# One arena on chip for the loads of a fused attention, soft-MoE and MLP kernel

## The chip, the cores and the metric

One core of a Trainium2 chip runs the whole kernel. The metric is the device time in microseconds (us), median of the runs. All inputs and outputs are float32 in device memory.

## The reference

The inputs q, k, v have 8 batches, 8 heads, 576 positions, 64 features; p has 32 rows a head. Three stages follow each other:

```
# stage 1, attention through 32 packed rows (per batch and head)
pp  = softmax(scale * p @ k.T) @ v
x   = softmax(scale * q @ pp.T) @ pp        # x becomes [4608, 512]
# stage 2, soft mixture of 8 experts with 4 slots each
L   = x @ phi                               # [4608, 32]
si  = softmax(L, over the 4608 rows).T @ x  # [32, 512]
so  = for each expert e:  relu(si[e] @ w1[e]) @ w2[e]   # w1 512x1024, w2 1024x512
y   = softmax(L, over the 32 slots) @ so    # [4608, 512]
# stage 3, MLP with mish
out = mish(y @ w_in) @ w_out                # w_in 512x2048, w_out 2048x512
```

## The kernel before, in words

**Stage 1** goes batch by batch. The half batches of k and q arrive as tiles of 128 x 1152 floats (4608 B a partition), are transposed by VectorE (`tr_kq`, L329 and L335) and freed; v is read by `pv`. The remainder of v, `vr` (L131), has two buffers of its own. The logits go into the tile LT, [128, 8, 192]. At the end of the stage the slot inputs stand in SIT (L949).

**Stage 2** runs the experts in order. `ex_h(e)` multiplies SIT with the four tiles of w1[e] (L981, 16 matmul records) and ScalarE copies the result (h, L988). `ex_x(e)` transposes it by TensorE (L996) and VectorE (h1T, L1000, relu L1001). `ex_o(e)` multiplies with the four tiles of w2[e] (L1008, 16 records). Between the experts stand the softmax over the slots (`combine`, VectorE, ScalarE and GpSimd, L1031 to L1049), its transposes into CS (`combine_t`, L1060 and L1065), a few idle matmuls `warm` (L975), and the conversion of w_in (`conv`, `convs`: ScalarE L274, VectorE L280 and L283). w_in and w_out are loaded as pairs of 32-bit words and turned into float32 on the chip, into `win[0..7]`. Eight tiles of w_in are loaded ahead of the experts (EARLY) and converted at the end of stage 1 (`bg`); four more are dealt out in the queue after w2 of expert 2, two after w1 of expert 3, two after w2 of expert 3; the sixteen tiles of w_out come last.

**Stage 3** first folds the expert outputs into the first MLP matrix (SOT, `emit_mp` L1149, `emit_mr` L1157, result MS). Then it takes blocks of 256 rows and quarters of the hidden width: `emit_h` (L1201) gives hidden values, ScalarE applies mish into tile `s` (L1206), the value is split into a high and a low part (`emit_c`, L1225 to L1236), and `emit_o` (L1316) multiplies with the split w_out (`whi`, `wlo`). Steps from the third block on use a Strassen-like form with sums S (L1217) and precomputed T tiles (`build_t`), and `emit_store` collects the result in `osb` (L1357, L1363). In the first six steps the last tiles of w_out are converted and split beside it (`cl`, `cu`, `cz`: L1186, L1187, L276).

**The order of the loads.** All loads are issued by SyncE's queue in the order of the list `jobs`: k, v, q and p, 8 early tiles of w_in, then the weights. `plan()` fixes for each job which ring it goes to, and `pump()` emits the next load as soon as the former owner of its buffer has been freed in the program text, so a load that waits holds up all behind it. Before the change there are five kinds of slots, all of 4608 B: ring_a (7), ring_b (20), ring_p (3, only in stage 1), and four slots of ring_x which belong to the transposed k and q until the last batch is done. A weight tile fills 4096 B of such a slot. The first weights take a7, b15, x4, b5, in this order, which is 31; the next one needs a tile that expert 0 has read. Ten of ring_b are used a second time; then ring_b and LT are given up (after `ex_o(4)`), and CS, MS, whi and wlo take their place. Each pool says whether a new tile waits for whole pools or for the tiles that it lies over (`reuse_waits="tile"`). The order of the instructions on each engine is the order of the program text (`manual_schedule`).

Of the kernel before, what the change touches and what calls it, by code (L numbers as in the profile page):

```python
# [9 lines left out]
F32 = mybir.dt.float32  # L10
F32R = mybir.dt.float32r
# [8 lines left out]
def kernel(  # L20
# [25 lines left out]
    FT = FF // 128  # L46
    TB = 4 * B
    RA, RB, RX, RP = 7, 20, 4, 3
    NE, NB2 = 8, 10
    NL = 16  # L50

    const = ctx.enter_context(tc.tile_pool(name="const", bufs=1))
    ring_a = ctx.enter_context(tc.tile_pool(name="ring_a", bufs=RA))
    wg = ctx.enter_context(tc.tile_pool(name="wg", bufs=4, reuse_waits="tile"))
    b_ctx, p1 = ExitStack(), ExitStack()
    ring_x = ctx.enter_context(tc.tile_pool(name="ring_x", bufs=RX // 2, reuse_waits="tile"))
    ring_b = b_ctx.enter_context(tc.tile_pool(name="ring_b", bufs=RB, side="right"))
    lt_p = b_ctx.enter_context(tc.tile_pool(name="lt_p", bufs=1, side="right"))
    ctx.enter_context(tc.manual_schedule())


    jobs = []
    CV = [("wi", i) for i in range(16)] + [("wo", i) for i in range(16)]
    N_CV = {(2, 1): 4, (3, 0): 2, (3, 1): 2}
# [6 lines left out]
    slots = {0: [ring_a, RA, []], 1: [ring_b, RB, []], 2: [None, RX // 2, []], 3: [None, RX // 2, []], 4: [None, RP, []]}  # L71
    got = {}
    freed = set()
    N_QKV = 3 * HQ * B + 1 + NE
    order = []

    def plan():

        n = RA + RB - NE + RP
        order.extend(0 if (i - N_QKV + RP) % (RA + RB) < RA else 1 for i in range(N_QKV))  # L80
        order[N_QKV - RP:N_QKV] = [4] * RP
        cycle = [2, 3] * (RX // 2) + [0] * RA
        rest = [0] * RA + [1] * (n - RA) + cycle[0:RX] + [1] * (NE - RP) + [0] * RA + [1] * NB2 + 9 * cycle
        late = len(AFTER[E - 1, 1])
        order.extend(rest[0:len(jobs) - late - N_QKV] + [0] * RA + [2, 3] * (RX // 2) + [0] * (late - RA - RX))

    nxt = [0]

    def pump():
        while nxt[0] < len(jobs):  # L90
            name, emit = jobs[nxt[0]]
            pool, n, held = slots[order[nxt[0]]]
            if pool is None or len(held) >= n and held[-n] not in freed:
                return
            t = pool.tile([128, 18 * D], F32, tag=("ring0", "ring1", "kT", "qT", "ring4")[order[nxt[0]]], name="r_" + "_".join(map(str, name)))
            held.append(name)
            got[name] = t
            emit(t)
            nxt[0] += 1
# [111 lines left out]
    slots[4][0] = p1.enter_context(tc.tile_pool(name="ring_p", bufs=RP))  # L211
# [45 lines left out]
    LT = lt_p.tile([128, B, 192], F32, name="LT")  # L257
# [602 lines left out]
    slots[2][0] = slots[3][0] = ring_x  # L860
# [98 lines left out]
    wg2 = wp.enter_context(tc.tile_pool(name="wg2", bufs=4, reuse_waits="tile"))  # L959
    t2 = wp.enter_context(tc.tile_pool(name="t2", bufs=2, reuse_waits="tile"))  # L960
    two = ep.enter_context(tc.tile_pool(name="two", bufs=2, reuse_waits="tile"))
    win += [wg2.tile([128, 1024], F32, name=f"win{i}", tag="wg") for i in range(4, 8)]
# [129 lines left out]
    convs((3, 1), 0, 2)  # L1092
# [43 lines left out]
    blk = {}  # L1136
# [54 lines left out]
    def emit_h(n, c, z):  # L1191

        if not z:
            blk["m", n, c] = tp.tile([128, 4, 256], F32, name="s", tag="s"), None
        if "Z" in R:
            hp = ps_b.tile([128, 512], F32, name="h3", tag="h3", bufs=2)
        else:
            hp = ps_h.tile([128, 2, 512], F32, name="h3", tag="hp")[:, 0]
        for f in range(2):
            ft = 4 * c + 2 * z + f  # L1200
            nc.tensor.matmul(  # L1201
                hp[:, 256 * f:256 * f + 256], lhsT=MS[:, 128 * ft:128 * ft + 128], rhs=CS[:, 256 * n:256 * n + 256],
                start=True, stop=True,
            )
        s = blk["m", n, c][0][:, 2 * z:2 * z + 2]
        nc.scalar.activation(out=s, in_=hp.rearrange("p (f n) -> p f n", f=2), func=AF.Mish)  # L1206
# [39 lines left out]
    def build_t(c, ws=None):  # L1246
# [21 lines left out]
        if ws is None:  # L1268
            wa, wb = (g2.tile([128, 1024], F32, name=x, tag=x, bufs=2).rearrange("p (f n) -> p f n", f=2) for x in tags)
# [15 lines left out]
        else:  # L1285
            T4 = tp.tile([128, 2, 256], F32, name="T4", bufs=1)
# [128 lines left out]
    tp = ctx.enter_context(tc.tile_pool(name="tp", bufs=2, side="right", reuse_waits="tile"))  # L1415
# [111 lines left out]
```

## Time and profile before

| | us |
|---|---|
| median of 3 runs | 657.84 |
| the 3 runs | 655.38, 659.72, 657.84 |
| span of the profiled execution, first to last instruction | 652.8 |
| median less that span | 5.04 |

| engine | busy in the span, us |
|---|---|
| TensorE matmul (PE) | 613.1 |
| TensorE weight load (PEld) | 529.8 |
| VectorE (DVE) | 503.1 |
| ScalarE (ACT) | 339.2 |
| GpSimd (POOL) | 57.4 |

The profile gives no device time of the profiled execution apart from its span, so what lies around the span is known only as the difference of the second table line. Times below are us from the start of the span. SP is SyncE, whose queue issues the loads. Stage 1 ends at about 162 us, the experts at about 222, and the long second MLP product begins at about 241.

### The profile page before, as it was taken

Reading aid. Unit: us, or ns where it says so; the run is one execution under the profiler, and the core shown is the slowest. Engines: PE = TensorE matmul, PEld = TensorE weight load, DVE = VectorE, ACT = ScalarE, POOL = GpSimd, SP = SyncE. Lnnn points to the kernel's source line nnn. Section 1 sums busy time; section 2 is a strip of 40 time slices with the busy share of each in tenths; the row PEclk is TensorE's granted clock in tenths of the full one; section 3 lists DMA queues with packets and bytes.
Section 4 is the critical chain, followed back from the end, with each engine's and each line's share of the span. In section 5 each row is a group of like instructions: output and inputs, shape, how many; then the busy total and the mean of one; then the engine's idle time right before and its main releaser. Section 6 shows DMA issues by size and latency. Waiting matters only on the chain.

```text
span 652.8 us, 14427 instructions
## 1 busy us (share of the span) xinstructions
PE 613.1 (94%) x5878; PEld 529.8 (81%) x5878; DVE 503.1 (77%) x997; ACT 339.2 (52%) x681; POOL 57.4 (9%) x78
## 2 busy tenths in 40 slices
PE   7799999998879969999999999999999999999996
PEld 5577777676225538888899999999999999999996
DVE  5998888787561298988779987788778877887883
ACT  3345545645522376655456555555555555555551
POOL 5122222121040040000000000000000000000000
PEclk9999999999979989999999999999999999999999
DMA  8998956998899980011100110111011101110111
GB/s 287 316 306 300 330 162 228 403 398 312 308 400 400 396 321 16 1 33 32 33 18 17 34 33 2 33 35 33 2 33 33 33 2 33 33 33 2 33 34 33
DMA packets 42354, 89.61 MB, mean 137 GB/s; under 512 B 10928, under 2 KB 19248, under 8 KB 42288
## 3 DMA queue, kind: packets, MB, share of 16 engines
q1 hardware_dynamic: 41840, 88.36, 38.9%
q8 instruction: 46, 0.75, 0.5%
q10 hardware_dynamic: 192, 0.26, 0.2%
q14 instruction: 20, 0.16, 0.1%
q0 software_dynamic: 256, 0.07, 0.0%
HBM read 79.23 MB, written 9.44 MB: 136 GB/s over the span
## 4 chain that ended last, share of the span: by engine, by line
PE 69%; DVE 18%; ACT 5%; DMA 5%; issue 2%; SPq 0%; POOL 0%; DVEq 0%; ACTq 0%; POOLq 0%
PE o L1316 39%; PE so L1316 13%; PE h L1201 5%; DVE kT L329 5%; DMA r_w<-in_moe_w_dram 3%; DVE A L501 1%; PE so L1008 1%; PE s L367 1%; DVE mx L500 1%; PE cp L1060 1%; PE s L481 1%; DVE osb L1357 1%; PE hp L981 1%; DVE nmx L377 1%; DVE S L1217 1%
## 5 line engine op out<-in xcount | busy, mean ns | idle before, releaser
L1316 PE MATMUL o<-whi,gh 128*128 128x256 f32 (+1 forms) x444 | 117.5, 309 | 0.5 <-DVE osb L1357 0.5
L1316 PE MATMUL o<-wlo,gh 128*128 128x256 f32 (+1 forms) x444 | 116.6, 307 | 0.0
L1232 ACT CAST gh<-s 128x512 fp32r<-128x512 f32 x116 | 53.8, 512 | 110.1 <-PE o L1316 110.1
L1206 ACT ACTIVATE s<-h 128x512 f32<-128x512 f32 x144 | 83.7, 595 | 45.3 <-PE h L1201 44.9
L1316 PE MATMUL o<-whi,gl 128*128 128x256 f32 (+1 forms) x444 | 95.6, 305 | 0.0
L1316 PEld LDWEIGHTS o<-wlo,gh 128*128 128x128 f32 x444 | 84.3, 190 | 4.7
L1316 PEld LDWEIGHTS o<-whi,gh 128*128 128x128 f32 x444 | 83.4, 190 | 5.3 <-issue 1.8
L1235 DVE TENSOR_TENSOR gl<-s,gh 128x512 fp32r<-128x512 f32 x116 | 59.5, 554 | 35.3 <-ACT gh L1232 35.3
L1236 DVE TENSOR_TENSOR Sl<-S,Sh 128x1024 fp32r<-128x1024 f32 x58 | 71.0, 1224 | 10.6 <-ACT Sh L1233 9.1
L1316 PEld LDWEIGHTS o<-whi,gl 128*128 128x128 f32 x444 | 71.6, 189 | 4.6
L1316 PE MATMUL o<-T,Sh 128*128 128x256 f32 x464 | 73.9, 281 | 0.4 <-DVE osb L1357 0.4
L1233 ACT CAST Sh<-S 128x1024 fp32r<-128x1024 f32 x58 | 61.0, 1052 | 5.4 <-DVE S L1217 4.1
L1316 PEld LDWEIGHTS o<-T,Sh 128*128 128x128 f32 x464 | 63.1, 188 | 0.6 <-DVE osb L1357 0.6
L1217 DVE TENSOR_TENSOR S<-s 128x256 f32<-128x256 f32 x116 | 48.8, 421 | 10.5 <-ACT s L1206 10.5
L1201 PE MATMUL h<-CS,MS 128*128 128x256 f32 x288 | 55.8, 284 | 0.0
L1316 PE MATMUL o<-T,Sl 128*128 128x256 f32 x232 | 46.9, 284 | 0.0
L1201 PEld LDWEIGHTS h<-CS,MS 128*128 128x128 f32 x288 | 44.1, 188 | 2.2 <-issue 1.0
L1357 DVE TENSOR_TENSOR osb<-osb,o 128x256 f32<-128x256 f32 x86 | 33.1, 418 | 9.6 <-PE o L1316 6.6
L1316 PE MATMUL so<-T,Sh 128*128 128x256 f32 (+1 forms) x232 | 38.6, 289 | 0.3 <-DVE osb L1357 0.3
L367 PE MATMUL s<-kT,win 128*128 128x288 f32 x128 | 34.7, 414 | 4.5 <-ACT win L379 4.0
L1316 PEld LDWEIGHTS o<-T,Sl 128*128 128x128 f32 x232 | 35.9, 190 | 0.0
L329 DVE STREAM_TRANSPOSE kT<-r_k 128x512 f32<-128x512 f32 x32 | 32.5, 1092 | 2.2 <-DMA r_k<-in_k_dram 2.2
(254 smaller groups left out, 1122.8 us busy)
## 6 DMA issues: line engine op xcount, KB each, us to landing
r_w<-in_moe_w_dram SPq DMA_DIRECT2D x63, 512.0 KB, 10.4
r_k<-in_k_dram SPq DMA_DIRECT2D x16, 576.0 KB, 7.3
r_q<-in_q_dram SPq DMA_DIRECT2D x16, 576.0 KB, 4.8
r_v<-in_v_dram SPq DMA_DIRECT2D x64, 128.0 KB, 5.7
r_wi<-in_moe_w_in_dram SPq DMA_DIRECT2D x16, 512.0 KB, 9.4
r_wo<-in_moe_w_out_dram SPq DMA_DIRECT2D x16, 512.0 KB, 8.5
out_dram<-osb SPq DMA_DIRECT2D x64, 128.0 KB, 2.2
vr<-in_v_dram SPq DMA_DIRECT2D x16, 64.0 KB, 2.7
```

Source lines behind the costliest of these rows:

```text
L329: nc.vector.transpose(out=T[:, dh, main].rearrange("p (i r a) -> p a i r" if nm == "k" else "p (i a r) -> p a i r", i=4, a=4,), in_=x[:, 0 ...
L367: nc.tensor.matmul(ps[:, n, 0:288], lhsT=pBD[b % 2][:, hq, dh], rhs=kT[:, dh, 288 * n:288 * n + 288], start=(dh == 0), stop=(dh == 1),)
L377: nc.vector.tensor_reduce(out=nmx, in_=ps[:, :, 0:288], axis=AX.XY, op=ALU.max, negate=True)
L1201: nc.tensor.matmul(hp[:, 256 * f:256 * f + 256], lhsT=MS[:, 128 * ft:128 * ft + 128], rhs=CS[:, 256 * n:256 * n + 256], start=True, stop=True,
L1206: nc.scalar.activation(out=s, in_=hp.rearrange("p (f n) -> p f n", f=2), func=AF.Mish)
L1217: nc.vector.tensor_tensor(out=S[:, k], in0=x, in1=y, op=op)
L1232: nc.scalar.copy(out=gh[:, f, t], in_=s[:, f, t])
L1233: nc.scalar.copy(out=Sh, in_=S)
L1235: nc.vector.tensor_tensor(out=gl[:, f, t], in0=s[:, f, t], in1=gh[:, f, t].bitcast(F32), op=ALU.subtract)
L1236: nc.vector.tensor_tensor(out=Sl, in0=S, in1=Sh.bitcast(F32), op=ALU.subtract)
L1316: nc.tensor.matmul(o, lhsT=lhsT, rhs=rhs, start=first, stop=stop)
L1357: add = lambda o, x, y: nc.vector.tensor_tensor(out=o, in0=x, in1=y, op=ALU.add)
```

## The change

q, k, v tiles, the weights and several buffers of the MLP are cut out of one pool `arena` with three tiles: AW (18 weight tiles, 72 KB a partition), AC (5) and AY (4856 floats, its tail holds LT). Tiles of q, k, v lie in it at a pitch of 4608 B, weights at a pitch of 4096 B; a load now waits until every earlier owner whose range it overlaps has been freed. ring_b, ring_p, lt_p, wg2 and p3 are gone; ring_a (7) and ring_x (4) stay. In stage 1 there are 29 slots (y2, c4, w16, a7). The first weights take y3, c5, w18, x4, a7: 37; the next ones c5 and then AW again. CS takes the place of AC; MS, whi and wlo that of AW (W3), after the experts. `win[4..7]`, the later `s` and `osb` tiles and T4 lie in AY. Since `win[4]` lies on the first weight tile, `ex_h(0)` now stands ahead of the first two conversions. All four tiles of w_in after expert 3's w1 follow at once, rather than two there and two after its w2. The tile pool `tp` serves only the first six steps of the MLP.

```diff
-    RA, RB, RX, RP = 7, 20, 4, 3
-    NE, NB2 = 8, 10
-    NL = 16
+    RA, RX, RW, RC, RY = 7, 4, 18, 5, 3
+    NE, NL = 8, 16
...
+    arena = ctx.enter_context(tc.tile_pool(name="arena", bufs=1, side="right", reuse_waits="tile"))
+    AW, AC, AY = (arena.tile([128, n], F32, name=x, tag=x) for x, n in (("AW", 1024 * RW), ("AC", 1024 * RC), ("AY", 4856)))
+    LT = AY[:, 4856 - 192 * B:4856].rearrange("p (b c) -> p b c", b=B)
-    N_CV = {(2, 1): 4, (3, 0): 2, (3, 1): 2}
+    N_CV = {(2, 1): 4, (3, 0): 4}
...
+        a, x = [("a", i) for i in range(RA)], [("x", i) for i in range(RX)]
+        first = [(z, 18 * D * i) for z, n in (("y", 2), ("c", 4), ("w", 16)) for i in range(n)] + a
+        order.extend(first[(i - N_QKV) % len(first)] for i in range(N_QKV))
+        y, c, w = ([(z, 1024 * i) for i in range(n)] for z, n in (("y", RY), ("c", RC), ("w", RW)))
+        order.extend((y + c + w + x + a + c + 2 * w)[0:len(jobs) - late - N_QKV] + (a + x + a)[0:late])
...
+            if any(k == kind and lo < at + n and at < hi and who not in freed for k, lo, hi, who in used):
+                return
...
-    win += [wg2.tile([128, 1024], F32, name=f"win{i}", tag="wg") for i in range(4, 8)]
+    win += [AY[:, 1024 * i:1024 * i + 1024] for i in range(4)]
...
+    ex_h(0)
     convs((2, 1), 0, 2)
-    ex_h(0)
...
-    convs((3, 1), 0, 2)
+    convs((3, 0), 2, 4)
...
-    b_ctx.close()
-    p3 = ctx.enter_context(tc.tile_pool(name="p3", bufs=1, side="right", reuse_waits="tile"))
-    CS = p3.tile([128, NT], F32R, name="CS")
-    MS = p3.tile([128, FF], F32R, name="MS")
-    whi = p3.tile([128, FT, DM], F32R, name="whi")
-    wlo = p3.tile([128, FT, DM], F32R, name="wlo")
+    CS = arena.tile([128, NT], F32R, name="CS", tag="AC")
...
+            s = tp.tile([128, 1024], F32, name="s", tag="s") if steps.index((n, c)) < 6 else two_of("s")
...
-            T4 = tp.tile([128, 2, 256], F32, name="T4", bufs=1)
+            T4 = AY[:, 4096:4608].rearrange("p (f n) -> p f n", f=2)
...
-            osb = g2.tile([128, 2, 512], F32, name="osb", tag="osb", bufs=2)
+            osb = two_of("osb").rearrange("p (z n) -> p z n", z=2)
...
-    tp = ctx.enter_context(tc.tile_pool(name="tp", bufs=2, side="right", reuse_waits="tile"))
+    W3 = arena.tile([128, 1024 * RW], F32R, name="W3", tag="AW")
+    whi, wlo = (W3[:, FT * DM * i:FT * DM * (i + 1)].rearrange("p (f n) -> p f n", f=FT) for i in range(2))
+    MS = W3[:, 2 * FT * DM:]
+    tp = wp.enter_context(tc.tile_pool(name="tp", bufs=2, reuse_waits="tile"))
+    turn = {"s": 0, "osb": 0}
+    def two_of(x):
+        turn[x] ^= 1
+        i = (0 if x == "osb" else 2048) + 1024 * turn[x]
+        return AY[:, i:i + 1024]
```

## Rows read from the trace of the kernel before

**Rows 1.** Stretches: length, busy us of each engine (instructions), granted clock, DMA share, GB/s.
```profile
162.00:222.00 60.00, 50.89 (x662) 21.68 (x664) 25.34 (x59) 19.27 (x32) 8.03 (x9) 0.94 0.97 365
242.00:652.80 410.80, 404.25 (x3052) 386.98 (x3050) 329.44 (x630) 225.40 (x386) 0.00 (x0) 0.99 0.10 25
```

**Rows 2.** Waits of the queues: engine, line, waited for: total us, times, longest; after 242 us.
```profile
PE o L1316 <- DVE osb L1357: 0.9, 3, 0.4
```

**Rows 3.** Stretch around the end of stage 1, columns as in rows 1.
```profile
156.00:172.00 16.00, 13.86 (x163) 6.58 (x167) 9.79 (x26) 6.56 (x15) 0.00 (x0) 1.00 0.65 224
```

**Rows 4.** Timeline of SyncE's queue, 150 to 190 us: start, us, what.
```profile
151.10 13.31 SPq L138 DMA_DIRECT2D r_w<-in_moe_w_dram  x4
165.73 5.77 SPq L148 DMA_DIRECT2D r_w<-in_moe_w_dram  x4
```

**Rows 5.** Waits of TensorE, 160 to 224 us, columns as in rows 2.
```profile
PE so L1008 <- DVE h1T L1001: 6.7, 2, 5.5
...
PE xp L996 <- ACT h L988: 0.8, 1, 0.8
...
PE hp L981 <- DMA r_w<-in_moe_w_dram: 0.2, 1, 0.2
```

**Rows 6.** Timeline of TensorE, 160 to 224.5 us; in brackets idle before and its end.
```profile
169.00 1.92 PE L1008 MATMUL so<-r_w,h1T 128*32 128x512 f32 x16
...
182.81 3.64 PE L1008 MATMUL so<-r_w,h1T 128*32 128x512 f32 x16 [5.47 <-DVE h1T L1001]
...
194.86 1.34 PE L981 MATMUL hp<-r_w,SIT 128*32 128x512 f32 x6
196.44 1.48 PE L981 MATMUL hp<-r_w,SIT 128*32 128x512 f32 x9 [0.24 <-DMA r_w<-in_moe_w_dram]
...
197.75 0.59 PE L981 MATMUL hp<-r_w,SIT 128*32 128x512 f32 x1
...
219.30 3.34 PE L1008 MATMUL so<-r_w,h1T 128*32 128x512 f32 x20
```

**Rows 7.** The chain that ended last, in order of time: start, us, what.
```profile
186.90 9.50 DMA r_w<-in_moe_w_dram
...
211.83 9.72 DMA r_w<-in_moe_w_dram
```

**Rows 8.** Timeline of ScalarE, 159 to 178 us.
```profile
160.09 1.24 ACT L274 ACTIVATE win<-r_wi 128x512 f32<-128x512 f32 x2
164.26 1.01 ACT L988 COPY h<-hp 128x1024 f32<-128x1024 f32 x1 [2.93 <-PE hp L981]
165.91 1.01 ACT L988 COPY h<-hp 128x1024 f32<-128x1024 f32 x1 [0.64 <-PE hp L981]
...
173.75 3.02 ACT L274 ACTIVATE win<-r_wi 128x512 f32<-128x512 f32 x4
```

**Rows 9.** Timeline of VectorE, 160 to 183 us.
```profile
162.00 0.76 DVE L280 TENSOR_SCALAR r_wi<-r_wi 128x512 int32<-128x512 int32 x2
162.67 1.29 DVE L283 SCALAR_TENSOR_TENSOR win<-win,r_wi 128x512 int32<-128x512 int32 x2
...
174.47 1.77 DVE L283 SCALAR_TENSOR_TENSOR win<-win,r_wi 128x512 int32<-128x512 int32 x2 [2.88 <-ACT win L274]
...
181.04 0.43 DVE L1000 STREAM_TRANSPOSE h1T<-xp 128x256 f32<-128x256 f32 x1
```

**Rows 10.** Waits of SyncE's queue, 80 to 105 us, columns as in rows 2.
```profile
SPq L131 <- PE pv L419: 12.4, 2, 9.6
```

**Rows 11.** Waits of TensorE, 222 to 242 us, columns as in rows 2.
```profile
PE mp L1157 <- DVE msb L1152: 5.2, 1, 5.2
```

**Rows 12.** Timelines of ScalarE and TensorE, 246 to 253 us.
```profile
247.53 1.14 ACT L1186 CAST whi<-w 128x512 fp32r<-128x512 f32 x2
...
248.47 1.10 PE L1316 MATMUL o<-whi,gl 128*128 128x512 f32 x4
```

**Rows 13.** Stretch of the first MLP steps, columns as in rows 1.
```profile
262.00:282.00 20.00, 20.00 (x93) 16.33 (x93) 19.25 (x32) 12.10 (x21) 0.00 (x0) 1.00 0.00 1
```

More of the change, by code (lines that the diff above doesn't have):

```diff
@@ L54 @@
     wg = ctx.enter_context(tc.tile_pool(name="wg", bufs=4, reuse_waits="tile"))
-    b_ctx, p1 = ExitStack(), ExitStack()
+    p1 = ExitStack()
     ring_x = ctx.enter_context(tc.tile_pool(name="ring_x", bufs=RX // 2, reuse_waits="tile"))
-    ring_b = b_ctx.enter_context(tc.tile_pool(name="ring_b", bufs=RB, side="right"))
-    lt_p = b_ctx.enter_context(tc.tile_pool(name="lt_p", bufs=1, side="right"))
+    arena = ctx.enter_context(tc.tile_pool(name="arena", bufs=1, side="right", reuse_waits="tile"))
     ctx.enter_context(tc.manual_schedule())
+    AW, AC, AY = (arena.tile([128, n], F32, name=x, tag=x) for x, n in (("AW", 1024 * RW), ("AC", 1024 * RC), ("AY", 4856)))
+    LT = AY[:, 4856 - 192 * B:4856].rearrange("p (b c) -> p b c", b=B)
     jobs = []
     CV = [("wi", i) for i in range(16)] + [("wo", i) for i in range(16)]
-    N_CV = {(2, 1): 4, (3, 0): 2, (3, 1): 2}
+    N_CV = {(2, 1): 4, (3, 0): 4}
     EARLY, CV = CV[:NE], CV[NE:]
@@ L70 @@
     assert len(CV) == NL
-    slots = {0: [ring_a, RA, []], 1: [ring_b, RB, []], 2: [None, RX // 2, []], 3: [None, RX // 2, []], 4: [None, RP, []]}
-    got = {}
-    freed = set()
     N_QKV = 3 * HQ * B + 1 + NE
@@ L77, in plan @@
     def plan():
[L79 to L83, printed above, removed]
-        late = len(AFTER[E - 1, 1])
-        order.extend(rest[0:len(jobs) - late - N_QKV] + [0] * RA + [2, 3] * (RX // 2) + [0] * (late - RA - RX))
+        late = len(AFTER[E - 1, 1])
+        a, x = [("a", i) for i in range(RA)], [("x", i) for i in range(RX)]
[3 more added lines that the diff above has]
+        order.extend((y + c + w + x + a + c + 2 * w)[0:len(jobs) - late - N_QKV] + (a + x + a)[0:late])
     nxt = [0]
+    used = []
+    freed = set()
+    got = {}
+    pool_x = []
     def pump():
         while nxt[0] < len(jobs):
-            name, emit = jobs[nxt[0]]
-            pool, n, held = slots[order[nxt[0]]]
-            if pool is None or len(held) >= n and held[-n] not in freed:
+            (kind, at), (name, emit) = order[nxt[0]], jobs[nxt[0]]
+            n = 1 if kind in "ax" else 18 * D if nxt[0] < N_QKV else 1024
+            if kind == "x" and not pool_x:
                 return
-            t = pool.tile([128, 18 * D], F32, tag=("ring0", "ring1", "kT", "qT", "ring4")[order[nxt[0]]], name="r_" + "_".join(map(str, name)))
-            held.append(name)
+            if any(k == kind and lo < at + n and at < hi and who not in freed for k, lo, hi, who in used):
+                return
+            used.append((kind, at, at + n, name))
+            nm = "r_" + "_".join(map(str, name))
+            if kind == "a":
+                t = ring_a.tile([128, 18 * D], F32, tag="ring0", name=nm)
+            elif kind == "x":
+                t = pool_x[0].tile([128, 18 * D], F32, tag=("kT", "qT")[at % 2], name=nm)
+            else:
+                t = {"w": AW, "c": AC, "y": AY}[kind][:, at:at + n]
             got[name] = t
@@ L210 @@
     one = p1.enter_context(tc.tile_pool(name="one", bufs=1))
-    slots[4][0] = p1.enter_context(tc.tile_pool(name="ring_p", bufs=RP))
     ps_s1 = p1.enter_context(tc.tile_pool(name="ps_s1", bufs=1, space=PSUM))
@@ L255, in consts2 @@
         nc.vector.tensor_copy(out=idrep.rearrange("p (g m) -> p g m", g=4), in_=ids[:, None, :].to_broadcast([128, 4, 32]))
-    LT = lt_p.tile([128, B, 192], F32, name="LT")
     nc.gpsimd.memset(LT, -1e30)
@@ L859 @@
     s2_mul(x, 1)
-    slots[2][0] = slots[3][0] = ring_x
+    pool_x.append(ring_x)
     pump()
@@ L958 @@
     so = ps_so.tile([128, DM], F32, name="so")
-    wg2 = wp.enter_context(tc.tile_pool(name="wg2", bufs=4, reuse_waits="tile"))
     t2 = wp.enter_context(tc.tile_pool(name="t2", bufs=2, reuse_waits="tile"))
     two = ep.enter_context(tc.tile_pool(name="two", bufs=2, reuse_waits="tile"))
-    win += [wg2.tile([128, 1024], F32, name=f"win{i}", tag="wg") for i in range(4, 8)]
+    win += [AY[:, 1024 * i:1024 * i + 1024] for i in range(4)]
     ex = {}
@@ L1193, in emit_h @@
         if not z:
-            blk["m", n, c] = tp.tile([128, 4, 256], F32, name="s", tag="s"), None
+            s = tp.tile([128, 1024], F32, name="s", tag="s") if steps.index((n, c)) < 6 else two_of("s")
+            blk["m", n, c] = s.rearrange("p (f n) -> p f n", f=4), None
         if "Z" in R:
@@ L1268, in build_t @@
         if ws is None:
-            wa, wb = (g2.tile([128, 1024], F32, name=x, tag=x, bufs=2).rearrange("p (f n) -> p f n", f=2) for x in tags)
+            wa, wb = (
+                (two_of(x) if x == "osb" else g2.tile([128, 1024], F32, name=x, tag=x, bufs=2)).rearrange("p (f n) -> p f n", f=2)
+                for x in tags
+            )
             B11, B12, B21, B22 = (w[:, :, 256 * j:256 * j + 256] for w in (wa, wb) for j in range(2))
```

## The prediction

> **What bounds the kernel now.** I read the stretches by stage first. In the long last one, 242 to 652.8 us, TensorE is busy 404 of 411 us and the transfers use a tenth of their engines [rows 1]; its largest single wait there is 0.9 us in total, on the output adds [rows 2]. So whatever the change saves before 242 us shifts this block as a whole, and inside it there is nothing for earlier loads to give. The change acts on the experts, 162 to 222 us. There the transfer engines are busy 97% at 365 GB/s while TensorE is busy 51 of 60 us [rows 1]. That looks like a stage bound by its loads. The waits say otherwise: in these 60 us TensorE lost 6.7 us to VectorE's relu (5.5 in one piece) and, as the view counts it, 0.2 us to a load [rows 5].
>
> **Where the loads stand still.** Between 156 and 172 us the transfer share is 0.65, that is 16 x 0.35 = 5.6 us without transfers [rows 3]. The queue shows why: the four tiles of expert 3's w1 take 13.3 us to issue, since the fourth, the 32nd weight tile, goes where a tile of expert 0 lies, and the four tiles of the w2 behind them take 5.8 us, waiting for the first `ex_o` [rows 4]. The change removes this first stop: tiles 32 to 37 find room earlier. The next stops follow in the code: the 38th tile lies on w1 tile 4 of expert 0, free when `ex_h(0)` has read it at about 164 us, where the copy of h begins [rows 8]; the 39th to 42nd lie on w2 of expert 0, free up to 165.73 + 5.77 = 171.5 us, the same moments at which the queue gets them today [rows 4]. At 512 KB a tile and the stage's 365 GB/s [rows 1] a tile is 1.4 us; the six extra tiles are 8.6 us of transfers, from about 162 on, and so last to about 170 or 171. The queue then runs nearly dry for 1 to 2 us, and I expect the loads from there on to land 4 to 5 us earlier, at most 5.6.
>
> **What of that reaches the path.** Two places. `ex_h(5)` is stretched by the last tile of its w1, issued at 186.90 and landing 9.50 us later at 196.40 [rows 7]: its 16 matmuls run from 194.86 to 197.75 + 0.59 = 198.34, or 3.48 us, where 16 matmuls of this form take 1.92 undisturbed, as at 169.00 [rows 6]. The wait view shows 0.24 us of this, because the matmuls in flight are drawn to their modelled ends. With the tile 4 us earlier the loss of 3.48 - 1.92 = **1.56 us** goes. What comes behind it is late by as much: the copy of h, the transposes of CS that wait for its buffer, and so on. The second place is w2 of expert 7, landing at 211.83 + 9.72 = 221.55 [rows 7]. The 20 matmuls there take 3.34 us, where 16 would take 1.92 and the four more about 0.43 at the same pace, 2.35 in all [rows 6]: at most 1.0 us is lost, at least nothing that is not the relu ahead of it. I take **0.3 us**, nearer to the small end, since the wait view gives loads 0.2 us in the whole stage [rows 5]. Both together are 1.86, with ends 1.5 and 2.6.
>
> The big hole is not a load's. `ex_o(2)` starts at 182.81 after 5.47 us of idling [rows 6], behind this line: ScalarE converts w_in from 173.75 [rows 8], VectorE's merge waits 2.88 us for it and begins at 174.47, then come the row sums of the slot softmax, two more conversions, and only at 181.04 the transpose of h1 of expert 2 [rows 9]. Nothing in this line waits for a load that the change moves, so it stays, and so do the slow matmuls behind it: the 16 at 182.81 take 3.64 us, where the same form takes 1.92 at 169.00 [rows 6].
>
> A rule of the Trainium skill would have it otherwise. "Perfetto Trace Analysis", section "Identifying the Most-Contended Engine", says to judge transfers by device memory utilization and to optimise the most contended engine first. By it the 365 GB/s of this stage [rows 1] would make the loads the bound, and the sum would be the whole 5.6 us. The trace does not agree so far: TensorE's waits in that stage are on VectorE.
>
> **What the change adds.** `ex_h(0)` now stands ahead of two conversions, because they write on the buffer that it reads. Before, ScalarE did the two in 1.24 us from 160.09, in the shadow of `ex_h`, and VectorE its four instructions, 0.76 + 1.29 = 2.05 us, from 162.00. Now they come between the copies of h of experts 0 and 1: the first copy ends at 164.26 + 1.01 = 165.27, the two conversions at 166.5, the second copy at 167.5, where it ends today at 165.91 + 1.01 = 166.92 [rows 8]. TensorE waits for this second copy already, 0.8 us [rows 5], so **0.5 us** more is on its path, and all the line behind moves with it. VectorE's part ends at about 167.3, and the transpose and relu of h1 of expert 0 follow it; `ex_o(0)`, which needs them, starts only at 169.00 [rows 6], behind the idle matmuls, so this is hidden. If the conversions ran twice as long, the cover would be gone. Bounds: 0 (the copy finds its place) to 1.24 (all of ScalarE's part).
>
> The rest I cost at nothing. The loads of q, k, v get 29 slots for 27, but the last stop of the queue there is `vr`, which waits 12.4 us for `pv` [rows 10] and keeps its two buffers. The 25th and 26th tile now wait for the first early conversion and tiles 31 to 37 for the others; all of these stand ahead of the two conversions at 160.09 on ScalarE [rows 8], when tiles before them are still on their way. The clearing and copying of `idm` lies over other stage 1 buffers; it is needed only when the first copy of h is done, after 165 [rows 8], and those buffers are last read before VectorE reaches 162.00 [rows 9]. Between 222 and 242 us the path is VectorE's (5.2 us of TensorE's wait end with its copy of msb [rows 11]), so w_out landing earlier buys nothing there. CS and W3 wait for tiles read well before.
>
> **Sum.** 0.5 - 1.56 - 0.3 = -1.36 us; on the span 652.8 this gives 651.4. The median of the runs is 657.84, 5.04 above the span, and I put that unchanged around it: **656.5 us**, 0.2% less. About 1%, 6.6 us, is what a measurement of this kernel can tell from no change; the three runs lie 4.3 us apart.
>
> **Rivals.**
> (a) *The stage is bound by its loads*, so the whole 5.6 us comes through: 652.2. For it speaks the transfer share of 0.97 [rows 1] and that TensorE reaches w2 of expert 7 just as it lands. Against it: TensorE's largest hole is VectorE's, and loads are named for 0.2 us [rows 5]. The engines' own line needs nearly the same time as the loads. Chance 0.12.
> (b) *The MLP's buffers get in each other's way.* With wg2 gone, T, Sh, Sl and S lie over the conversion buffers of w_out, whose last readers are the copies and splits of the first seven steps; a first write that waits for those stalls VectorE. At 262 to 282 us it is busy 19.25 of 20 us [rows 13], so only 0.75 us of a stall is hidden, and TensorE is at 20.00. One copy pair of ScalarE is 1.14 us [rows 12]; one to three of them in VectorE's way are 1.1 to 3.4 us, less the 0.75. Above 1.36 + 0.75 = 2.1 us of stall the kernel is slower than before: at three, 656.5 + 2.7 = 659.2. Against it: by the code the readers stand ahead of these writes. Chance 0.10.
> (c) *The arena is tracked whole*, so that a matmul on one weight waits for loads far ahead of it, and the change does the opposite of what it says. From the second turn of AW on, each `ex_h` would wait about 18 tiles of 1.4 us, 25 us once: some 680. Against it: today ScalarE writes one part of whi at 247.53 while TensorE still has reads of another part before it in the text, at 248.47 [rows 12], so parts of a tile are told apart. Chance 0.03.
> (d) *Nothing arrives*: the loads gain, but what goes at `ex_h(5)` comes back as another wait of the engines' line, and with the 0.5 us the time is 658.3. Chance 0.12.
>
> My forecast has the remaining 0.63. Its own range is 656.5 with the bounds of the terms (2.6 gained and nothing added, to 1.5 gained and 1.24 added, so 655.2 to 657.6) and the runs' spread, about 2 to each side: 653.5 to 659.5. The range for 8 in 10 takes in most of (a) and (b), **652.0 to 659.8**. Faster by over 1% (below 651.3) is left with the far end of (a): 0.06. Slower by over 1% (above 664.4) is (c) and mishaps of that size: 0.06. Within 1%: 0.88.
>
> **What would show it.** In the profile after, the stretch 156 to 172 has a transfer share near 0.95; the queue's long issue moves to w2 of expert 3. `ex_h(5)` takes about 1.9 us, with no load in TensorE's waits; the hole ahead of `ex_o(2)` is still there, near 5.5 us and 0.5 us later; the second copy of h ends near 167.5. The first matmul of the second MLP product begins 1 to 2 us earlier than today, and the block behind it is as long as before. I am wrong if the hole ahead of `ex_o(2)` shrinks or grows by more than 1 us, if the clock behind it changes, or if the block after 242 us changes its length.

## The result

The changed kernel took **651.02 us** (median of five runs, 647.56 to 652.52) against 655.38 of before in the same session (five runs, 655.16 to 659.72; the 657.84 of the table ahead is the median of the first three of them). The ratio estimated from the runs is 0.9899, 95% interval 0.9864 to 0.9933; the quotient of the two medians is 0.9933. Run again (a2) it took 649.37 us against 657.36, ratio 0.9887 (0.9848 to 0.9927). So it is about 1% faster; the prediction had 0.2% and a range that ended at 652.0.

The stretches of the changed kernel, as in [rows 1, 3] (columns: the stretch, its length, busy time of PE, PEld, DVE, ACT, POOL with instructions, granted clock, DMA share, GB/s):
```profile
core 0 of [0], span 648.5 us
156.00:172.00 16.00, 13.51 (x161) 6.96 (x164) 9.64 (x26) 6.93 (x16) 0.00 (x0) 1.00 0.83 327
162.00:222.00 60.00, 51.19 (x681) 22.60 (x681) 25.99 (x62) 20.40 (x36) 7.98 (x9) 0.94 0.98 383
242.00:648.50 406.50, 399.77 (x3052) 382.74 (x3050) 328.70 (x630) 224.69 (x386) 1.99 (x1) 1.00 0.10 26
```
The transfers fill 156 to 172 us better (0.83 for 0.65), and the last stretch, in which nothing waits for a load in either kernel, is shorter: 406.5 us for 410.8 [rows 1].

SyncE's queue, which answers to [rows 4] (start, us, what):
```profile
161.67 0.38 SPq L155 DMA_DIRECT2D r_w<-in_moe_w_dram  x1
164.92 7.19 SPq L155 DMA_DIRECT2D AC<-in_moe_w_dram  x3
```
The long stop is now at the w2 of expert 3, which has to wait for the tiles of expert 0.

TensorE in the experts, as in [rows 6]:
```profile
170.15 1.92 PE L1012 MATMUL so<-AC,h1T 128*32 128x512 f32 x16
183.38 3.64 PE L1012 MATMUL so<-AW,h1T 128*32 128x512 f32 x16 [4.89 <-DVE h1T L1005]
195.34 1.90 PE L985 MATMUL hp<-AW,SIT 128*32 128x512 f32 x16
```
`ex_h(5)` is one piece of 1.90 us where it was three that spanned 3.48 [rows 6]. The hole ahead of `ex_o(2)` is still there, 4.89 us for 5.47, and so is the slow `ex_o(2)` behind it.

ScalarE, as in [rows 8]:
```profile
164.99 1.01 ACT L992 COPY h<-hp 128x1024 f32<-128x1024 f32 x1 [4.00 <-PE hp L985]
165.89 1.27 ACT L279 ACTIVATE AY<-AW 128x512 f32<-128x512 f32 x2
167.07 1.00 ACT L992 COPY h<-hp 128x1024 f32<-128x1024 f32 x1
```
The two conversions now stand between the two copies of h.

**Where the time went.** Three rows cut both kernels at the same work: the copies of SIT (end of stage 1) and of SOT (end of the experts) on VectorE, and the first `emit_h` of the fourth step of the MLP (a step is one block of 256 rows and one quarter of the hidden width). Before:
```profile
161.80 0.29 DVE L949 COPY SIT<-sit_ps 128x128 f32<-128x128 f32 x1 [0.55 <-PE sit_ps L943]
225.89 0.29 DVE L1413 COPY SOT<-sot_ps 128x128 f32<-128x128 f32 x1 [1.20 <-PE sot_ps L1406]
252.22 0.40 PE L1201 MATMUL h<-CS,MS 128*128 128x256 f32 x2
```
After:
```profile
162.59 0.29 DVE L954 COPY SIT<-sit_ps 128x128 f32<-128x128 f32 x1 [0.56 <-PE sit_ps L948]
224.13 0.29 DVE L1416 COPY SOT<-sot_ps 128x128 f32<-128x128 f32 x1 [2.37 <-PE sot_ps L1409]
252.16 0.39 PE L1201 MATMUL h<-CS,W 128*128 128x256 f32 x2
```
With the spans of 652.83 and 648.48 us the four parts are, before and after: stage 1 161.80 and 162.59 (+0.79), experts 64.09 and 61.54 (**-2.55**), the first MLP product with the steps begun beside it, called the first product below, 26.33 and 28.03 (+1.70), and the rest of the MLP, called the block below, 400.61 and 396.32 (**-4.29**). Together -4.35. The experts gained 2.55 us and lost 2.49 around them; what shows in the total is the block.

### The profile page after: what moved, and what is told of

The parts are those of the page before. It is cut to its first block, busy times and chain, and to the rows that moved or that the text cites. A ratio compares the mean times of both kernels' runs of the same rounds, so it can differ in the third digit from the quotient of the medians.

```text
span 648.5 us, 14426 instructions
## 1 busy us (share of the span) xinstructions
PE 610.3 (94%) x5878; PEld 527.1 (81%) x5878; DVE 502.2 (77%) x997; ACT 337.9 (52%) x681; POOL 57.2 (9%) x78
## 4 chain that ended last, share of the span: by engine, by line
PE 73%; DVE 18%; ACT 4%; DMA 2%; issue 2%; SPq 0%; POOL 0%; DVEq 0%; ACTq 0%; POOLq 0%
PE o L1319 39%; PE so L1319 13%; PE h L1201 5%; DVE kT L334 4%; PE so L1012 2%; PE hp L985 2%; DVE A L506 1%; PE s L372 1%; PE cp L1064 1%; DVE mx L505 1%; PE s L486 1%; DVE AY L1360 1%; DVE S L1217 1%; DVE nmx L382 1%; DMA AC<-in_k_dram 1%
## 5 line engine op out<-in xcount | busy, mean ns | idle before, releaser
L1319 PE MATMUL o<-W,gh 128*128 128x256 f32 (+1 forms) x888 | 159.4, 306 | 0.5 <-DVE AY L1360 0.5
L1319 PEld LDWEIGHTS o<-W,gh 128*128 128x128 f32 x888 | 129.7, 190 | 10.0 <-issue 1.9
L1232 ACT CAST gh<-AY 128x512 fp32r<-128x512 f32 x116 | 53.8, 512 | 108.9 <-PE o L1319 108.9
L1206 ACT ACTIVATE AY<-h 128x512 f32<-128x512 f32 x132 | 77.0, 593 | 37.8 <-PE h L1201 36.4
L1319 PE MATMUL o<-W,gl 128*128 128x256 f32 (+1 forms) x444 | 94.5, 303 | 0.0
L1235 DVE TENSOR_TENSOR gl<-AY,gh 128x512 fp32r<-128x512 f32 x116 | 59.4, 554 | 32.9 <-ACT gh L1232 32.9
L1319 PEld LDWEIGHTS o<-W,gl 128*128 128x128 f32 x444 | 70.9, 189 | 4.5
L1217 DVE TENSOR_TENSOR S<-AY 128x256 f32<-128x256 f32 x116 | 48.8, 421 | 9.9 <-ACT AY L1206 9.9
L1201 PE MATMUL h<-CS,W 128*128 128x256 f32 x288 | 55.7, 284 | 0.0
L1201 PEld LDWEIGHTS h<-CS,W 128*128 128x128 f32 x288 | 43.9, 188 | 2.2 <-issue 1.0
```

What stands on the lines that cost most here:

```text
L1201: nc.tensor.matmul(hp[:, 256 * f:256 * f + 256], lhsT=MS[:, 128 * ft:128 * ft + 128], rhs=CS[:, 256 * n:256 * n + 256], start=True, stop=True,
L1217: nc.vector.tensor_tensor(out=S[:, k], in0=x, in1=y, op=op)
L1232: nc.scalar.copy(out=gh[:, f, t], in_=s[:, f, t])
L1235: nc.vector.tensor_tensor(out=gl[:, f, t], in0=s[:, f, t], in1=gh[:, f, t].bitcast(F32), op=ALU.subtract)
L1319: nc.tensor.matmul(o, lhsT=lhsT, rhs=rhs, start=first, stop=stop)
```

## The experiments

The same cut for every kernel that ran whole, in us (first lines of the experiments' sections say what each is; "tiles" are the weight tiles ahead; "W" is where whi, wlo, CS and MS start, "left" where T, gh, gl, Sh and Sl start, both as the remainder of their SBUF address by 256 bytes, read from the program):

| kernel | tiles | W, left | stage 1 | experts | first product | block | `ex_h(5)` |
|---|---|---|---|---|---|---|---|
| before | 31 | 224, 64 | 161.80 | 64.09 | 26.33 | 400.61 | 3.49 |
| after | 37 | 0, 64 | 162.59 | 61.54 | 28.03 | 396.32 | 1.90 |
| a2 (after again) | 37 | 0, 64 | 163.03 | 61.12 | 25.93 | 396.34 | 1.90 |
| e1 | 31 | 128, 64 | 163.95 | 65.57 | 25.69 | 399.46 | 3.56 |
| e2 | 37 | 32, 64 | 162.11 | 62.14 | 27.89 | 400.42 | 1.90 |
| e3 | 31 | 0, 64 | 163.75 | 64.02 | 27.85 | 396.33 | 3.76 |
| e4 | 37 | 128, 128 | 164.25 | 61.98 | 27.87 | 402.64 | 1.90 |
| e6 | 37 | 0, 64; T 128, CS 64 | 163.51 | 61.14 | 25.88 | 391.46 | 1.90 |
| e7 | 31 | 0, 64 | 161.56 | 65.77 | 28.06 | 396.43 | 5.27 |

The theory after the first comparison: the block got shorter because its matmuls found their operands at other addresses in SBUF, since its steps grew shorter one like the other: a step, from its first `emit_h` to that of the next, takes 5.48 us before and 5.41 after (mean of 42 between 400 and 634 us). The matmuls tell the same by their operands. From one start to the next (mean over 400 to 600 us, worked out from the starts in the traces), those of `whi` with gl take 117.2 ns before and 113.3 after; those of T with Sh, which both keep their remainder of 64, take 118.2 and 118.4. Rivals: the loads, or the place of the buffers at large. The first guess was too narrow: multiples of 128 bytes.

**e1, the kernel before with a pad of 96 bytes.**
```diff
     wlo = p3.tile([128, FT, DM], F32R, name="wlo")
+    pad = p3.tile([128, 24], F32, name="pad")
```


> The kernel before with one unused tile of 96 bytes a partition behind wlo, so that CS, MS, whi and wlo (and the s and T4 tiles below them) start at multiples of 128 bytes instead of 96 past one; loads, order and buffers stay. Theory A (the matmuls of the MLP stream whi and wlo faster where these start at multiples of 128 bytes): the stretch from 243 us to the end is 409.8 us long before and 405.5 us in the changed kernel, so it becomes 405 to 406.5 us; the time comes to 651 to 652 us, ratio to before 0.993 to 0.995; in the W-by-gl matmuls of 400 to 600 us the mean interval from start to start falls from 117 to 113.5 ns. Theory B (the earlier loads and the emptier queue make the difference): nothing moves, 655.4 us within 0.3. Theory C (the new places of s, osb, T4 and S, Sh, Sl in the arena make it): nothing moves, 655.4 us.


Measured: 655.44 us, ratio 0.9968 (0.9939 to 0.9996); block 399.46. The 1.1 us lie in the first steps of the block; a later step stays at 5.48, and `whi` with gl at 117.6 ns where theory A had 113.5. Multiples of 128 are not it.

**e2, the changed kernel with its arena 32 bytes on.**
```diff
-    ... (("AW", 1024 * RW), ("AC", 1024 * RC), ("AY", 4856))
-    LT = AY[:, 4856 - 192 * B:4856]
+    ... (("AW", 1024 * RW), ("AC", 1024 * RC), ("AY", 4848))
+    LT = AY[:, 4848 - 192 * B:4848]
```


> The changed kernel with AY 8 words shorter, so that the whole arena (W3 with whi, wlo and MS, CS, and AY) starts 32 bytes past a multiple of 128; everything else stays. Theory A (start addresses at multiples of 128 bytes): the stretch from 243 us on goes back from 405.5 us to 409 to 410 us, the time to 654 to 655.5 us, ratio to before 0.998 to 1.000. Theories B (loads) and C (which buffer lies where, in rough terms): 651 us within 0.5, ratio 0.990 to 0.993.


Measured: 653.85 us, ratio 0.9926 (0.9899 to 0.9952). The block is back at 400.42 by 32 bytes alone, with `W` and gl at 117.4 ns again, while the experts keep their 62.14. So loads and rough places are out as causes of the shorter block. The time came out between the theories: it keeps what the experts gain.

**e3, the changed kernel with 31 tiles ahead.**
```diff
-        order.extend((y + c + w + x + a + c + 2 * w)[0:len(jobs) - late - N_QKV] + ...
+        order.extend((c + w[0:15] + x + a + c + 2 * w)[0:len(jobs) - late - N_QKV] + ...
```


> The changed kernel with 31 weight tiles ahead instead of 37 (the three slots of AY and three of AW are left out of the first pass), the addresses of the MLP as in the changed kernel. Theory A: the MLP's stretch stays at 405.5 us and the time within 1 us of the changed kernel's 651.0; the six tiles are worth what arrived early of them, 0 to 0.6 us. Theory B: the MLP's stretch goes back to 409.8 us and the time to 655.


Measured: 652.41 us, ratio 0.9916 (0.9883 to 0.9948). The block stays at 396.33; the experts are back at 64.02. The six tiles are worth more than I allowed: the five profiles with 37 have 61.1 to 62.1 us of experts, the four with 31 have 64.0 to 65.8. The row that does it, in e3 (TensorE's timeline):
```profile
196.69 1.67 PE L985 MATMUL hp<-AW,SIT 128*32 128x512 f32 x6
198.54 1.47 PE L985 MATMUL hp<-AW,SIT 128*32 128x512 f32 x9 [0.19 <-DMA AW<-in_moe_w_dram]
199.86 0.59 PE L985 MATMUL hp<-AW,SIT 128*32 128x512 f32 x1
```
It is the torn `ex_h(5)` of [rows 6], 3.76 us long, in a kernel that differs from the changed one in its tiles ahead alone.

**e4, all of the left side 64 bytes on, the arena 128.**
```diff
+    pad_c = const.tile([128, 16], F32, name="pad_c")
     half_c = const.tile([128, 1], F32, name="half_c")
```
(and AY 4824 floats long in place of 4856)


> The changed kernel with everything on the left side of SBUF (T, gh, gl, S, Sh, Sl, s, which start at 64 past multiples of 128 bytes) moved by 64 bytes, to multiples of 128; the arena moves by 128 bytes and stays at multiples of 128. Theory A1 (each operand counts, and needs 128): the matmuls with T or Sh, Sl, some 60 in 100 of the 3060, whose intervals are 117 to 120 ns, go toward 113.5, 4 to 5 ns each or 7 to 9 us in all: 642 to 645 us, ratio to before 0.980 to 0.984. Theory A2 (64 bytes are enough, T and the rest have that now and their intervals have another cause, the traffic of VectorE and ScalarE beside them): 651 us within 0.5. Theory C (where the buffers lie at large): 651 us.


Measured: 656.41 us, ratio 0.9962 (0.9939 to 0.9985); block 402.64, a step 5.55 us. Both versions of the theory missed: with every operand at multiples of 128 the block is the slowest of all. What counts is how the operands stand to each other.

**m1, matmuls alone.** The core of it:
```diff
+    for a, m in enumerate(MV):          # streamed operand: bytes past a multiple of 1024
+        for b, w in enumerate(WT):      # weights
+            for r in range(6):
+                six(o[:, 0:256], m, w, ...)
```


> Matmuls alone: none of the computation of the reference is in it, its output is a constant. 100 blocks of 36 matmuls of the MLP's shape (128x128 weights, 256 columns, float32r) in the MLP's order of hi and lo, no other engine beside them; from block to block only the start address of the streamed operand (0, 32, 64, 96, 128, 256, 384, 512, 896, 992 bytes past a multiple of 1024) and of the weights (0, 64, 128, 192, 256, 320, 384, 512, 832, 896) changes. Theory D (the pace goes by the start addresses of the two operands, of the one against the other): the 36 of a block take 36 x 113.3 ns = 4.08 us with 0 and 320 or 832 as in the changed kernel, 36 x 118 = 4.25 us with 992, 32 or 896 and 320 or 832, 36 x 120 = 4.32 us with 128 and 384 or 896. Theory E (the pace goes by what VectorE and ScalarE read and write beside them): all blocks take the same, 4.08 us.


Four of its blocks in TensorE's timeline: streamed and weights at 0 and 0, 0 and 320, 32 and 0, 64 and 0:
```profile
47.44 4.48 PE L37 MATMUL zb<-big 128*128 128x256 f32 x36
68.83 4.26 PE L37 MATMUL za<-big 128*128 128x256 f32 x36
90.04 4.37 PE L37 MATMUL zf<-big 128*128 128x256 f32 x36
132.61 4.24 PE L37 MATMUL zd<-big 128*128 128x256 f32 x36
```
The same 36 matmuls take 4.48 or 4.24 us with no other engine at work. From one block's start to the next, by 36, in ns (four of the ten rows, named by the streamed operand's bytes; columns: the weights'; the very last block, 992 and 896, by its 35 intervals):
```
        0     64    128    192    256    320    384    512    832    896
  0  119.9  117.8  118.8  117.8  120.0  113.9  118.6  119.8  117.8  119.0
 64  113.3  119.9  117.9  118.8  117.8  120.0  113.8  113.3  119.9  117.9
128  118.6  117.8  120.0  113.9  118.5  117.8  120.0  119.8  117.8  120.0
992  118.4  118.7  119.8  116.7  118.4  118.6  119.8  118.4  118.7  119.9
```
Over all 100 blocks, equal remainders by 128 give 118.5 to 120; 64 apart gives 113.3 to 113.9 in 7 blocks and about 117.8 in the other 23; 32 off gives 116.7 to 120.1. Theory E is out, and the exact form of D too: of pairs that are 64 apart some run fast and some don't (0 and 320 do, 256 and 320 don't), and the pace found after the first few matmuls holds for the block. Of the pairs foreseen, 992 with 320 took 118.6 (118 expected), but 0 with 832 117.8 (113.3 expected).

**m2, four steps of the MLP replayed** with the addresses of each kernel.
```diff
+    for name, addr, delta in LAYOUTS:
+        for i, ((m, w, b, c, wide), (am, aw)) in enumerate(zip(OPS, addr)):
+            x, y = (am + delta.get(m, 0) - BASE) // 4, (aw + delta.get(w, 0) - BASE) // 4
+            nc.tensor.matmul(dst, lhsT=at_(y, 128), rhs=at_(x, 256), ...)
```


> Matmuls alone: none of the reference is computed, the output is a constant. 184 matmuls of the MLP (four of its steps) are replayed in their order with the SBUF addresses that streamed operand and weights have there, no other engine beside them, in 20 layouts: of the kernel before, of the changed kernel, of the padded before (e1), the arena 32 bytes on (e2), the left side 64 bytes on (e4), and the changed one with T, CS or both moved by 64 bytes, the latter also in variants by multiples of 64, 128 and 256. In the kernels' own traces four such steps take 21.92 us before, 21.63 in the changed kernel, 21.93 in e1, 21.94 in e2 and 22.20 in e4. Theory D (the operands' addresses alone set it): the replays give these within 0.1 us and in this order; with T and CS both 64 bytes off their weights' residue by 128 all matmuls can run at 113.3 ns and four steps take 20.9 to 21.3 us. Theory E (traffic of the other engines): the layouts take the same time, about 20.9 us.


TensorE's timeline, one row a layout: before, after, e1's, e2's and e4's, before moved by 992 bytes to a multiple of 1024, and after with T, with CS, with both 64 bytes on, and with T 192 and CS 64 bytes on:
```profile
31.80 22.05 PE L56 MATMUL before<-big 128*128 128x256 f32 x184
53.91 21.86 PE L56 MATMUL after<-big 128*128 128x256 f32 x184
75.82 22.18 PE L56 MATMUL bpad<-big 128*128 128x256 f32 x184
98.06 22.14 PE L56 MATMUL shift<-big 128*128 128x256 f32 x184
120.25 22.45 PE L56 MATMUL left<-big 128*128 128x256 f32 x184
142.76 21.89 PE L56 MATMUL bup<-big 128*128 128x256 f32 x184
164.70 21.84 PE L56 MATMUL tup<-big 128*128 128x256 f32 x184
186.59 21.82 PE L56 MATMUL csup<-big 128*128 128x256 f32 x184
208.47 21.53 PE L56 MATMUL tcs<-big 128*128 128x256 f32 x184
230.06 22.01 PE L56 MATMUL tcsb<-big 128*128 128x256 f32 x184
```
The replay separates the kernels as their traces do: after is the fastest of the five, e4's the slowest, the other three lie between; it is 0.1 to 0.3 us longer than four steps in the kernels (21.92 before, 21.63 after), so theory D's 0.1 us was too tight, and of the 0.29 us between before and after it shows 0.19. The same layout comes out the same: after, and after with T and CS moved, stand in it twice, 21.86 and 21.86, 21.53 and 21.54. With both moved, theory D had 20.9 to 21.3 us; 21.53 misses that. In the layout with T and CS moved, 256 or 512 bytes more on one operand change the time by at most 0.02 us (21.51 to 21.54), 128 more on T cost 0.48. So the remainder by 256 bytes is what counts here, and T and CS have something left to give.

**m3, 64 layouts.** As m2, two steps each, with gh, gl, then Sh, Sl, then T at 0, 64, 128 and 192 by 256.


> Matmuls alone: none of the reference is computed, the output is a constant. 92 matmuls (two steps of the MLP) are replayed for each of 64 layouts, in which the start addresses of gh and gl, of Sh and Sl, and of T take the residues 0, 64, 128 and 192 by 256 bytes, with W and MS at 0 and CS at 64. Theory D: a layout's time goes by these residues; 92 matmuls at 113.3 ns would be 10.4 us, at 120 ns 11.0 us. The layout of the changed kernel with T and CS moved (gh and Sh at 64, T at 128) took 21.6 us for four steps, so 10.7 to 10.8 us here; others come to between 10.5 and 11.1 us. Theory E (other causes): all layouts take the same time.


The shortest, one with gh, Sh and T all at 64, and the longest:
```profile
281.13 11.00 PE L52 MATMUL gbbc<-big 128*128 128x256 f32 x92
269.98 11.10 PE L52 MATMUL gbbb<-big 128*128 128x256 f32 x92
145.60 11.38 PE L52 MATMUL gacc<-big 128*128 128x256 f32 x92
```
The layout of e6 came out at 11.00 us where 10.7 to 10.8 was expected, and the longest 0.3 above its bound, but a spread is there, 0.4 us. The shortest is gh and Sh at 64, T at 128: m2's best, and what e6 builds.

**e6, the changed kernel with T and CS moved.**
```diff
+    const.tile([128, 16], F32, name="pad_c")                        # ring_a (T) to 128 by 256
     ring_a = ...
+    ctx.enter_context(tc.tile_pool(name="pad1", bufs=1)).tile([128, 48], F32, name="pad_g")   # gh, gl stay at 64
     wg = ...
+    ctx.enter_context(tc.tile_pool(name="pad2", bufs=1)).tile([128, 16], F32, name="pad_x")   # ring_x (T) to 128
     ring_x = ...
-    CS = arena.tile([128, NT], F32R, name="CS", tag="AC")
+    CS = arena.tile([128, NT + 16], F32R, name="CS", tag="AC")[:, 16:]
-                t = g2.tile([128, 1280], F32, name="T", bufs=1)
+                t = g2.tile([128, 1328], F32, name="T", bufs=1)[:, 0:1280]
```
(and AY 4728 floats long, so that the arena still starts at a multiple of 256)


> The changed kernel with T 64 bytes on (128 past multiples of 256, where its weights Sh and Sl are at 64) and CS at 64 (its weights, in MS, at 0); gh, gl, Sh, Sl stay at 64 and whi, wlo at 0 past multiples of 256. In the replay this layout took 21.58 us for four steps of the MLP against 21.91. Theory D: about 38 steps with 0.08 us less each, 3 us: 647 to 649 us, ratio to before 0.984 to 0.989, and 5.32 to 5.34 us for a step in the trace in place of 5.41. Theory E: 651 us, as the changed kernel.


Measured: **643.95 us, ratio 0.9785 (0.9745 to 0.9824)**: faster than both kernels, and below the 647 to 649 expected. The block is 391.46, a step 5.31 us: 0.095 us less a step where the replay had 0.08, and 4.9 us less in the block where 3 was expected. Here T with Sh goes from 118.4 to 116.0 ns, while `W` with gl, which this edit does not touch, stays at 113.4. The profiled run also has one of the short first products (25.88), on which more below. The stretch 400 to 600 us, in which TensorE never stops, counts it; first before, then after, then e6:
```profile
400.00:600.00 200.00, 200.00 (x1682) 199.58 (x1681) 157.95 (x320) 110.52 (x192) 0.00 (x0) 1.00 0.10 25
```
```profile
400.00:600.00 200.00, 200.00 (x1704) 199.62 (x1704) 160.03 (x324) 112.51 (x195) 0.00 (x0) 1.00 0.10 25
```
```profile
400.00:600.00 200.00, 200.00 (x1734) 199.63 (x1733) 164.24 (x334) 114.07 (x198) 0.00 (x0) 1.00 0.10 26
```
1682, 1704 and 1734 matmuls of the same forms in the same time, at the same full clock and the same DMA share.

**e7, the kernel before with a pad of 224 bytes.** As e1, with `[128, 56]`.


> The kernel before with one unused tile of 224 bytes behind wlo: CS, MS, whi and wlo start at multiples of 256 bytes, where T, gh, gl, Sh and Sl are at 64, as in the changed kernel; the loads and everything else are those of before. Theory D (the residues by 256 bytes of streamed operand and weights set the pace; the pad of 96 had put W at 128 by 256): a step of the MLP takes 5.41 us in place of 5.48, the MLP from 252 us on is 3.5 to 4.5 us shorter, the time 4 us below before on the same chip, ratio 0.992 to 0.995. The stretch up to the copy of SOT stays as before (about 64 us from the copy of SIT). Rival (the arena as a whole, or the loads, are needed): ratio 0.998 to 1.000.


Measured: 653.71 us, ratio 0.9943 (0.9913 to 0.9972). The block is 396.43 and 400 to 600 us holds 1704 matmuls:
```profile
core 0 of [0], span 651.8 us
400.00:600.00 200.00, 200.00 (x1704) 199.62 (x1704) 159.73 (x323) 112.33 (x195) 0.00 (x0) 1.00 0.10 25
```
An unused tile gives the kernel before the whole of the block's gain, and `whi` with gl its 113.3 ns, with no load moved. The experts were not as before (65.77): `ex_h(5)` took 5.27 us here, so with 31 tiles its loss is not one fixed size.

**e8, the first conversions ahead of `ex_h(0)` again.**
```diff
-    ex_h(0)
     convs((2, 1), 0, 2)
+    ex_h(0)
     ex_h(1)
```


> The changed kernel with the first pair of conversions for the arena back ahead of the first product of expert 0, as before; loads and addresses stay. The prediction put 0.5 us on the second copy of h in the other order. If that is on the path, the first product of expert 1 starts 0.35 us sooner and the copy of SOT, seen from the copy of SIT, with it (61.0 us in place of 61.3), time 0.3 to 0.5 us less; if the wait ahead of the third second product takes it back, as the traces suggest, the copy of SOT comes 61.3 us after that of SIT, within 0.3, and the time is that of the changed kernel within 0.5 us.


Measured: 652.05 us, ratio 0.9922 (0.9895 to 0.9949). It can't answer its question: the conversions write over the slot in which expert 0's w1 lies, so expert 0's first product starts 1.37 us behind the end of the copy of SIT in place of 0.06, and is computed from the converted tiles. It and that of expert 1 together span 164.57 to 171.09 us, 6.52 in place of 3.64, at a granted clock of 0.57 (163 to 171 us). The block is that of after (396.33).

**a2, the changed kernel once more**, beside e7.


> The changed kernel once more, on the same chip as the two others: ratio to before 0.987 to 0.993; a step of the MLP 5.41 us, the copy of SOT 61.0 to 61.5 us after that of SIT.


Measured: 649.37 us, ratio 0.9887 (0.9848 to 0.9927). Both gains are there again, and the first product takes 25.93 us.

## Why the prediction was wrong

**The step that failed** is its third sentence: whatever the change saves before 242 us "shifts this block as a whole, and inside it there is nothing for earlier loads to give". The second half is right; the first was taken from the wait view [rows 2], which can't speak of the pace of an engine that never waits. The sum had this block at nothing; it gave 4.29 us in the profiled pair, more than all terms together. The change moved `whi`, `wlo`, CS and MS from a remainder of 224 to 0 by 256 bytes, and the matmuls that read `whi` and `wlo` got shorter (117.2 to 113.3 ns with gl); those of T with Sh, neither of which moved, did not (118.2 and 118.4). e2 takes the gain away with 32 bytes, e7 gives it to the kernel before. No rival had it.

**The level.** The forecast of 656.5 stood on 657.84, with 5.04 us around the span. A run's time is about 1.8 us above its own span (650.29 and 648.5 in the profiled run of after); the other 3.2 were the distance from the median of three runs to a profiled run that was faster. Of the 5.5 us by which 656.5 missed 651.02, 2.5 are this level (655.38 for 657.84), and 3.0 are the change (4.36 for 1.36).

**ScalarE's order, +0.5.** The delay is there: from the start of `ex_h(0)` to that of `ex_h(2)` it is 8.95 us in place of 8.60. But it doesn't reach `ex_o(2)`, which stands 20.50 us behind the end of the copy of SIT (20.72 before): the hole ahead of it, put down to VectorE, shrank from 5.47 to 4.89. I had the hole as fixed and the delay as added to it; it was slack for what comes earlier. In all six profiles with the new order `ex_o(2)` starts 20.49 to 20.58 us behind the copy of SIT, in the three with the old one 20.71 or 20.72. e3, with the new order and 31 tiles, gives 64.02 us of experts against 64.09: the order costs nothing that shows. Why it gains 0.2 was not tried.

**`ex_h(5)`, -1.56.** Right in place and size: 3.49 to 1.90, and 1.90 in all five profiles with 37 tiles.

**w2 of expert 7, -0.3.** Right in place and size. The 20 matmuls at 219.30 are 8 of expert 6 and 12 of expert 7, whose last quarter is computed in another form behind them. Before, the last four of the 20 start at 221.59, just behind the landing at 221.55; after, the 20 take 2.99 us for 3.34, and the `so` matmuls of both experts 4.30 for 4.65. The 2.35 that the prediction set for the 20 is not reached: what stands between them was not all a load's.

The experts' sum was -1.36; measured -2.55, of which 1.59 and 0.35 are these last two, 0.22 is the stretch up to `ex_o(2)`, and 0.39 lies in small pieces between. Over all profiles the means are 64.86 us with 31 tiles (four) and 61.58 with 37 (five), 3.3 apart: the profiled run of before was at the kind end.

**Why the first pair hid it.** The first product of the MLP takes 25.7 to 26.3 us in four profiles and 27.9 to 28.1 in five, of both kinds of kernel (e7 among the long ones, a2 and e6 among the short). In all nine the granted clock falls from 2.4 to 1.2 GHz once in the stretch from 235 to 249 us. The long ones, and none of the short, have one more fall between 224 and 234 us: in sum TensorE is at the lower level for 10.2 us of this stage in the five and for 6.8 in the four (the traces' records of the clock). Before, then after, then a2, with the granted clock third from the right; the lines at 18 us are from stage 1:
```profile
18.00:24.00 6.00, 6.00 (x46) 5.46 (x48) 5.97 (x9) 1.10 (x4) 2.11 (x4) 1.00 1.05 344
224.00:230.00 6.00, 5.62 (x61) 3.51 (x60) 3.00 (x8) 3.89 (x9) 0.00 (x0) 1.00 1.02 407
```
```profile
18.00:24.00 6.00, 5.19 (x23) 4.44 (x24) 5.86 (x10) 1.84 (x6) 1.96 (x4) 0.72 1.03 364
224.00:230.00 6.00, 5.62 (x45) 2.44 (x44) 2.92 (x7) 2.94 (x7) 0.00 (x0) 0.72 1.03 412
```
```profile
224.00:232.00 8.00, 7.44 (x62) 3.33 (x61) 6.03 (x12) 6.28 (x13) 0.78 (x1) 1.00 1.02 409
```
TensorE had been busy nearly all the time before in after and in a2 (23.17 and 23.56 of 24 us from 200 to 224 us), and only after has the fall there. The fall comes and goes between executions of the same program, and in both kinds of kernel, so nothing here makes it a cost of the change. Why the clock falls there is open; it wasn't tried. Stage 1 goes the same way: 161.6 to 162.1 us in the three profiles without a fall in it, 162.6 in after with 3.4 us at the lower level, 163.0 to 164.3 in the five with 6.8.

**The rivals.** (a), bound by loads, got nearest in time (652.2), but for another reason, so by luck: the loads landed 4.9 us earlier (the last of w2 of expert 7 at 218.03 for 222.90), and 2.55 came through, not 5.6. (b) and (c) did not happen. (d) is refuted by the table: `ex_h(5)` gives its gain in all five. The signs named at the end held for the queue, `ex_h(5)`, the hole (within 1 us) and the second copy of h, seen from the end of stage 1; the transfer share is 0.83, not 0.95; the second MLP product begins 0.2 us earlier (240.63 for 240.84), not 1 to 2, while in a2, without the further fall of the clock, it begins at 239.16; and the last one, a block that changes its length, is the one that came.

## What to carry to other kernels

Where an engine runs without a pause, look at its pace, not at its waits: equal matmuls whose means go from 113 to 121 ns with their operands in one steady stretch (after, 400 to 600 us) are a sign that something other than their columns sets it. A change of buffers is a change of addresses; print them before and after, and replay the steady part alone with either set before looking for causes in the schedule. And cut two traces at the same work, stage by stage, on more than one execution: here a gain of 2.55 us in one stage was covered by a clock that fell in those around it.

## What was not expected of the hardware

A matmul of 256 columns whose weights are loaded beside it took 113.3 to 120.1 ns where nothing but the start addresses of its two SBUF operands changed (m1), and of the layouts of one MLP step the best is 4.3% shorter than the worst (5.31 in e6, 5.55 in e4). Which of two paces a pair that is 64 bytes apart falls into is open: 0 and 320 and 256 and 320 both ran behind a pair of equal remainder, at 113.9 and 117.8, and no run here tells the exact addresses from what ran before. Why the addresses count at all is not shown either.

The Trainium skill, "SBUF — State Buffer", section "A bandwidth-pool intuition that's wrong (but worth ruling out)", gives the weight loads a second, independent read port. m1 doesn't show two reads that are independent of each other: with no other engine at work and the weights at 0, the streamed operand at 0 takes 119.9 ns and at 64 takes 113.3. The page of the Trainium skill "TensorE: Matmul & The Clock Gate", section "Back-to-back issue gap", says that in a stream of weight loads and matmuls both set the spacing. m1 agrees: with the streamed operand at 0, moving the weights alone takes it from 113.9 to 120.0 ns. The runs add that it goes by where both lie.
